# Two chained attentions and a mixture of four networks: PSUM in one pool of four double banks, sums of products made by a unit of their own, attention early in each pair, first loads reordered

## The chip, the cores and the metric

The kernel runs on one core of one Trainium2 chip. The time is device microseconds (us), the median of three runs. Beside it there is one profiled execution, from which all durations are read. A core has five engines with a queue each: TensorE (PE in the profile; its weight loads are PEld), VectorE (DVE), ScalarE (ACT), GpSimd (POOL) and SyncE (SP, which here only issues DMAs). Each engine works through its own queue in order.

## The reference

Eight batches of eight heads with 576 tokens of 64 values each. A packed attention of 32 queries `p` over `k` and `v` gives 32 packed rows per head; the tokens `q` then attend to these rows, which are keys and values at once. The result, as a matrix `x` of 4608 x 512, goes through four two-layer networks weighted per token:

```python
p_packed = sm_attn(p, k, v)
out = sm_attn(q, p_packed, p_packed)
...
p = domain_probs / (domain_probs.sum(-1, keepdims=True) + 1e-09)
for e in range(E):
    h = np.maximum(x @ w1[e], 0.0)
    out += p[:, e:e + 1] * (h @ w2[e])
```

Everything is float32. D is 512, the hidden width F is 1024, E is 4.

## The kernel before

**Units.** Batches go in four pairs (`sb`). The hidden widths of the four networks are cut into eight channels of 512 (`ch`). A unit is one channel of one batch, 64 in all, in the order pair, channel, even batch, odd batch. The loop at the end runs over them.

**A unit.** Its main work is seven products (`product`, `ORDER`): h @ w2 with hidden blocks and weights combined by Strassen-Winograd rules, so that seven products of blocks replace eight. A product is 12 matmuls of 288 columns into a double PSUM bank. Float32 precision comes from splitting each operand into a rounded part (hi, an ACT cast) and a rest (lo, a POOL subtraction), and three matmuls per block. Four groups of 12 matmuls (`mm1_group`) make the hidden blocks `ablk` of the next unit; DVE takes them out of PSUM with the relu and the token's weight (L299). `s_operand` makes the combined blocks `sblk` (DVE, L316) and the split operand `st`, two products ahead. Each product is taken out of PSUM by DVE and added to one of seven sums `acc` (L382), in channel 0 copied by ACT (L380).

**The end of a pair.** In the last channel `finish` (L391) also combines the seven sums to the four blocks of the output: seven additions of two sums each, all on DVE and right behind the product that they need, and four stores.

**Attention.** `pack_unit` (two pairs of heads of the packed attention; four packs per pair of batches) loads k and v, makes scores on PE (`kt,pbd`), the maximum on DVE (L158), the exponential on ACT (L162), transposes it on PE (L70), multiplies with v (`vt,at`), scales (L188), transposes (`ident,ppn`) and writes the packed rows `ppbd`. `tok_unit` (also four per pair) makes the tokens' scores (`kt,ppbd`), a softmax over 32 entries on DVE and ACT (L219 to L233), and the split result `xh`, `xl`. Attention of the next pair runs beside the units of this pair: packs in the even units of channels 1 to 4, tokens in the even units of channels 5 and 6 and in both units of channel 7. `g_form` multiplies w1 with the packed rows (`wraw,ppbd`), so that mm1 needs only the attention weights `xh`, `xl`.

**First pair.** `t_form` makes the combined and split blocks of w2 of the next channel in the odd units of the first pair, and `t_store` puts them into DRAM; later pairs load them back. Before the loop, attention of batches 0 and 1, the first w1 and w2 and the first mm1 run as a start-up.

**PSUM.** Eight banks: three double buffers `dbl` (mm1, products, scores) and two single buffers `aux` (transposes, products with v, g_form).

**Order.** The program is recorded in the order of the code; a scheduler with a simulated timeline then sets the order of each engine's queue. `together` forces the matmuls of one g_form behind all PE work recorded before it.

Of the kernel before, what the change touches and what calls it, by code (L numbers as in the profile page):

```python
# [16 lines left out]
P = 128  # L17
# [21 lines left out]
def attention_moe(ctx: ExitStack, tc: tile.TileContext, q, k, v, p, dp, w1, w2, out):  # L39
# [7 lines left out]
    xpool = pool("xpool", 3)  # L47
# [4 lines left out]
    ps_aux = pool("ps_aux", 2, space=PSUM)  # L52
    ps_dbl = pool("ps_dbl", 3, space=PSUM)
# [28 lines left out]

    def aux():
        return ps_aux.tile([P, 512], F32, name="aux")
# [32 lines left out]
    def norm_probs():  # L117
        pb = const.tile([P, E, TP], F32, name="pb")
        nc.sync.dma_start(out=pb, in_=dp)
# [7 lines left out]
        nc.sync.dma_start(out=pnd.rearrange("e (p t) -> p e t", p=P), in_=pb)  # L127

    def pack_unit(b, g, new):
        pd = pbd[b % 2]  # L130
        if g == 0:
            pt = small.tile([P, NPAIR, NPK], F32, name="pt", bufs=1)
            nc.sync.dma_start(out=pt, in_=p[b])
            for hh in range(2):
                nc.gpsimd.tensor_copy(
                    out=pd[hh * D:(hh + 1) * D, :, hh * NPK:(hh + 1) * NPK], in_=pt[hh * D:(hh + 1) * D]
                )
        kt = new([P, 2, S], "kt")
        nc.sync.dma_start(out=kt, in_=k[b][:, 2 * g:2 * g + 2, :])
        vt = new([P, len(SC), 4 * D], "vt")  # L140
# [30 lines left out]
        ps = aux()  # L171
        for c in range(nfull):
            tr(out=ps[:, c * P:(c + 1) * P], in_=a1[:, c * P:(c + 1) * P], identity=ident)
        nc.scalar.copy(out=at[:, 0:nfull, :], in_=ps.rearrange("p (c s) -> p c s", s=P))
        ps = aux()
        r = S - nfull * P
        tr(out=ps[0:r, 0:P], in_=a1[:, nfull * P:S], identity=ident)
        nc.scalar.copy(out=at[0:r, nfull, :], in_=ps[0:r, 0:P])
        yield
        ps = aux()  # L180
        for c, (_, n) in enumerate(SC):
            for h in range(4):
                mm(
                    out=ps[h * NPK:(h + 1) * NPK, 0:D], lhsT=at[0:n, c, h * NPK:(h + 1) * NPK],
# [3 lines left out]
        nc.vector.tensor_scalar_mul(ppn, ps[:, 0:D], rs)  # L188
        yield
        ps = aux()  # L190
        tr(out=ps[0:D, 0:P], in_=ppn, identity=ident)
        psv = ps[0:D, 0:P].rearrange("p (j h n) -> p j h n", j=2, h=2)
# [9 lines left out]
    def tok_unit(b, g, new):  # L202
# [20 lines left out]
        nc.vector.tensor_tensor(out=a2, in0=a2, in1=m2.broadcast_to([P, S // 32, NPK]), op=ALU.subtract)  # L223
# [6 lines left out]
        nc.vector.tensor_tensor(out=a2, in0=a2, in1=s2.broadcast_to([P, S // 32, NPK]), op=ALU.mult)  # L230
# [18 lines left out]
    def g_form(bs, ch, raws):  # L249

        for g in range(NG):
            pss = {b: aux() for b in bs}
# [11 lines left out]
            for b in bs:  # L264
                ghl = gpool.tile([P, 2, FC], F32R, name="ghl", bufs=6)
# [68 lines left out]
    def t_form(ch, new, eng):  # L334
# [15 lines left out]
        for i, name in enumerate(ORDER):  # L350
            n = of[name]
            if n in how:
                t = new([P, 2, DH], {"t1": "at", "t2": "a1", "t3": "a1", "t4": "at"}[n])
                eng.tensor_tensor(out=t, in0=blk[how[n][0]], in1=blk[how[n][1]], op=ALU.subtract)
# [9 lines left out]
    def product(u, i):  # L364
# [16 lines left out]
        elif ch < NCH - 1:  # L381
            nc.vector.tensor_tensor(out=accs[b, i], in0=psv, in1=accs[b, i], op=ALU.add)  # L382
        else:
            finish(b, ORDER[i], psv)

    def finish(b, name, psv):
# [6 lines left out]
        def store(t, r, n):  # L393
            nc.sync.dma_start(
                out=out[n * DH:(n + 1) * DH, b * S + r * HS:b * S + (r + 1) * HS].rearrange("(j p) t -> p j t", p=P),
                in_=t,
            )

        t = m[name]
        if name == "a22":  # L400
            add(t, m["s3"], t, ALU.subtract)
            add(t, t, psv, ALU.subtract)
            store(t, 1, 0)
# [5 lines left out]
        elif name == "s2":  # L409
# [4 lines left out]
            store(m["s1"], 1, 1)  # L414
        elif name == "s4":
            store(t, 0, 1)
        elif name == "a12":
            store(t, 0, 0)
# [26 lines left out]
    with ExitStack() as first:  # L445
# [10 lines left out]
        toks = [tok_unit(b, g, unit_tile(2 * b + g)) for b in range(2) for g in range(NG)]  # L456
        forms = t_form(0, form_tile, nc.gpsimd)
        for i in range(2):
            next(packs[i])
        raws = w1_load(0)  # L460
        for i in range(2):
            next(packs[i])
        for i in range(2):
            next(toks[i])
        for i in range(2, 4):
            next(packs[i])
        norm_probs()
        next(forms)
        drain(wavefront(packs[:2], 1))
        for b in range(2):  # L470
            load_probs(b, 0)
        drain(g_form([0], 0, raws))
        drain(wavefront(toks[:2], 1))
# [97 lines left out]
```

## Time and profile before

| | |
|---|---|
| median of 3 runs | 1380.16 us (1379.9 to 1381.48) |
| the profiled execution's own time | 1386.64 us |
| its span, first to last instruction | 1384.9 us |
| DVE, ACT, POOL busy | 71%, 34%, 58% of the span |
| DMA | 208.92 MB, 44.5% of 16 engines on the hardware queue |

All terms below are of the profiled execution, which took 6.5 us longer than the median of the other runs; its time lies 1.7 us above its span. A line of the profile names the source line (L67 is the helper that records every matmul), the engine, the operation, what it writes and reads, and how often. Names in brackets behind a row give the idle time before it and what ended it. L67, L70 and L75 are helpers, so that the tile names tell groups apart: `dbl<-st,tt` is a product, `dbl<-xl,ghl` and `dbl<-xh,ghl` are mm1, `aux<-wraw,ppbd` is g_form. PE is clocked down at times: PEclk is the share of full speed.

### The profile page before, as it was taken

To read this page: it belongs to the slowest core of one execution; us is meant where nothing else is said; L and a number is where in the kernel's file an instruction comes from. 1 tells how busy PE (TensorE), PEld (TensorE's weight loads), DVE (VectorE), ACT (ScalarE), POOL (GpSimd) and SP (SyncE) were. 2 spreads that over 40 slices of the span, in tenths; PEclk is the share of its full clock that TensorE was granted. 3 is DMA by queue.
4 is the path that set the end of the run, shared out by engine and by line. 5 is a ranking of instruction groups with operands and counts; after the bars stand their busy time and mean duration, and the time that the engine had idled before them with its cause. 6 is when DMAs were issued, how large, how long until landed. Compare 5 with 4: busy or idle time off the path is not lost.

```text
span 1384.9 us, 26088 instructions
## 1 busy us (share of the span) xinstructions
PE 1312.6 (95%) x10464; PEld 1192.3 (86%) x10464; DVE 984.0 (71%) x1380; ACT 475.0 (34%) x786; POOL 804.0 (58%) x548
## 2 busy tenths in 40 slices
PE   5699999999889999999998999999998899999997
PEld 2488898888888889899987998889997799999997
DVE  4757778788994666667798466666779656666668
ACT  2354343434325333233323433333332342332331
POOL 2656887777846445555645544455565455555555
PEclk9789999999999999999999999999999999999999
DMA  8525454444553444444445443445444344443421
GB/s 279 209 94 176 169 183 168 166 166 143 182 188 122 144 145 158 157 159 144 132 152 174 133 164 135 133 139 163 148 146 151 111 145 132 146 146 131 138 92 69
DMA packets 84630, 208.92 MB, mean 151 GB/s; under 512 B 8608, under 2 KB 27168, under 8 KB 84512
## 3 DMA queue, kind: packets, MB, share of 16 engines
q1 hardware_dynamic: 84512, 207.27, 44.5%
q8 instruction: 83, 1.36, 0.4%
q14 instruction: 35, 0.29, 0.1%
HBM read 168.37 MB, written 38.87 MB: 150 GB/s over the span
## 4 chain that ended last, share of the span: by engine, by line
PE 76%; DVE 16%; DMA 3%; issue 2%; POOL 1%; ACT 1%; DVEq 0%; SPq 0%; ACTq 0%
PE dbl L67 71%; DVE acc L391 5%; PE aux L75 4%; DVE sblk L316 4%; DVE ablk L299 2%; DMA kt<-in_w 1%; DVE ghl L115 1%; DVE acc L382 1%; DVE a L223 1%; DMA pb<-in_dp 1%; POOL xl L115 1%; PE aux L70 1%; DMA kt<-in_q 1%; DVE s L227 0%; DVE a L219 0%
## 5 line engine op out<-in xcount | busy, mean ns | idle before, releaser
L67 PEld LDWEIGHTS dbl<-st,tt 128*128 128x128 f32 x5376 | 736.1, 189 | 93.1 <-issue 61.4
L67 PE MATMUL dbl<-st,tt 128*128 128x288 f32 x5376 | 791.3, 299 | 23.2 <-DVE acc L391 6.6
L115 POOL TENSOR_TENSOR st<-sblk,st 128x576 fp32r<-128x576 f32 x256 | 397.7, 1559 | 292.3 <-ACT st L110 288.5
L67 PE MATMUL dbl<-xh,ghl 128*128 128x288 f32 x2048 | 419.8, 297 | 0.0
L115 POOL TENSOR_TENSOR st<-ablk,st 128x576 fp32r<-128x576 f32 x192 | 286.3, 1491 | 228.4 <-ACT st L110 193.1
L67 PEld LDWEIGHTS dbl<-xh,ghl 128*128 128x128 f32 x2048 | 333.4, 191 | 0.0
L299 DVE SCALAR_TENSOR_TENSOR ablk<-dbl,pbt 128x576 f32<-128x576 f32 x256 | 192.6, 752 | 188.8 <-PE dbl L67 188.7
L67 PE MATMUL dbl<-xl,ghl 128*128 128x288 f32 x1024 | 306.5, 299 | 17.3 <-POOL xl L115 15.5
L382 DVE TENSOR_TENSOR acc<-dbl,acc 128x576 f32<-128x576 f32 x336 | 253.2, 754 | 90.3 <-PE dbl L67 89.4
L110 ACT CAST st<-sblk 128x576 fp32r<-128x576 f32 x256 | 173.0, 676 | 356.3 <-DVE sblk L316 232.3
L110 ACT CAST st<-ablk 128x576 fp32r<-128x576 f32 x192 | 129.7, 675 | 261.6 <-PE dbl L67 241.2
L67 PEld LDWEIGHTS dbl<-xl,ghl 128*128 128x128 f32 x1024 | 195.2, 191 | 20.1 <-POOL xl L115 16.7
L316 DVE TENSOR_TENSOR sblk<-ablk 128x576 f32<-128x576 f32 x128 | 116.0, 906 | 10.7 <-POOL st L115 0.5
L115 DVE TENSOR_TENSOR ghl<-aux,ghl 128x512 fp32r<-128x512 f32 x128 | 83.3, 684 | 53.1 <-ACT ghl L110 53.1
L75 PE MATMUL aux<-wraw,ppbd 64*32 64x512 f32 x1024 | 85.9, 621 | 1.9 <-DVE ppbd L195 1.8
L110 ACT CAST ghl<-aux 128x512 fp32r<-128x512 f32 x128 | 69.0, 588 | 49.9 <-PE aux L75 49.9
L316 DVE TENSOR_TENSOR sblk<-ablk,sblk 128x576 f32<-128x576 f32 x64 | 65.4, 1022 | 6.5 <-POOL st L115 0.8
L391 DVE TENSOR_TENSOR acc<-acc,acc 128x576 f32<-128x576 f32 x56 | 58.1, 1069 | 0.2
L316 DVE TENSOR_TENSOR sblk<-sblk,ablk 128x576 f32<-128x576 f32 x64 | 55.7, 871 | 2.0
L380 ACT COPY acc<-dbl 128x576 f32<-128x576 f32 x56 | 35.7, 639 | 57.3 <-PE dbl L67 57.3
L391 DVE TENSOR_TENSOR acc<-dbl,acc 128x576 f32<-128x576 f32 x48 | 35.4, 742 | 1.7 <-PE dbl L67 1.7
L75 PEld LDWEIGHTS aux<-wraw,ppbd 64*32 64x32 f32 x1024 | 14.3, 106 | 23.4 <-issue 15.5
(66 smaller groups left out, 496.2 us busy)
## 6 DMA issues: line engine op xcount, KB each, us to landing
tt<-td SPq DMA_DIRECT2D x168, 512.0 KB, 3.8
wraw<-in_w SPq DMA_DIRECT2D x128, 256.0 KB, 3.0
td<-tt SPq DMA_DIRECT2D x56, 512.0 KB, 2.6
kt<-in_k SPq DMA_DIRECT2D x16, 576.0 KB, 3.8
kt<-in_q SPq DMA_DIRECT2D x16, 576.0 KB, 3.6
pbt<-pnd SPq DMA_DIRECT2D x32, 288.0 KB, 3.9
out<-acc SPq DMA_DIRECT2D x32, 288.0 KB, 2.6
vt<-in_v SPq DMA_DIRECT2D x16, 512.0 KB, 3.8
```

The source lines that it names most:

```text
L67: on_pe(nc.tensor.matmul(**kw))
L70: on_pe(nc.tensor.transpose(**kw))
L75: ins = nc.tensor.matmul(**kw).ins
L110: nc.scalar.copy(out=dst, in_=src)
L115: eng.tensor_tensor(out=dst, in0=src, in1=hi.bitcast(F32), op=ALU.subtract)
L223: nc.vector.tensor_tensor(out=a2, in0=a2, in1=m2.broadcast_to([P, S // 32, NPK]), op=ALU.subtract)
L299: nc.vector.scalar_tensor_tensor(out=a, in0=ps[:, :, 0:HS], scalar=0.0, in1=pbt[b][:, ts].rearrange("p (o t) -> p o t", o=1).broadcast_to( ...
L316: nc.vector.tensor_tensor(out=t, in0=blk(x), in1=blk(y), op=op)
L380: nc.scalar.copy(out=accs[b, i], in_=psv)
L382: nc.vector.tensor_tensor(out=accs[b, i], in0=psv, in1=accs[b, i], op=ALU.add)
L391: nc.vector.tensor_tensor(out=dst, in0=x, in1=y, op=op)
```

## The change

- PSUM: one pool of four double buffers for everything. The transposes of one pack go into one of them, and both batches of one g_form share one; the split results `ghl` have five buffers in place of six.
- `finish` stays for the last batch alone. All others only add their products, and `combine` makes the seven additions of two sums, three on DVE and four on POOL, one behind each product of the unit that follows in the code.
- Attention: in the first pair one pack or token unit in every even unit (packs in channels 0 to 3, tokens in channels 4 to 7); in the second and third pair one in every unit from the third to the tenth. `x` has four buffers in place of three.
- g_form runs one product later, behind the mm1 group of that product. Of the first unit, the mm1 groups for unit 1 come behind products 4 to 6.
- Start-up: the token weights are normed first, their DMAs on ACT's queue; k of both packs ahead of v, w2 ahead of w1; the copies into `pbd` on ACT in place of POOL; one token unit's subtraction and scaling on POOL.
- `t_form`: the first of four subtractions of a channel on POOL in place of DVE.

```diff
-    ps_aux = pool("ps_aux", 2, space=PSUM)
-    ps_dbl = pool("ps_dbl", 3, space=PSUM)
+    ps_dbl = pool("ps_dbl", 4, space=PSUM)
...
     def norm_probs():
-        nc.sync.dma_start(out=pb, in_=dp)
+        nc.scalar.dma_start(out=pb, in_=dp)
...
     def pack_unit(b, g, new):
-                nc.gpsimd.tensor_copy(
+                nc.scalar.copy(
...
         nc.sync.dma_start(out=kt, in_=k[b][:, 2 * g:2 * g + 2, :])
+        yield
...
     def g_form(bs, ch, raws):
-            pss = {b: aux() for b in bs}
+            ps = dbl()
+            pss = {b: ps[:, b % 2] for b in bs}
...
     def product(u, i):
-        elif ch < NCH - 1:
+        elif ch < NCH - 1 or b < B - 1:
             nc.vector.tensor_tensor(out=accs[b, i], in0=psv, in1=accs[b, i], op=ALU.add)
         else:
             finish(b, ORDER[i], psv)
...
+    def combine(b):
+        m = {n: accs[b, i] for i, n in enumerate(ORDER)}
+        for eng, dst, x, y, op, to in (
+            (nc.vector, "s2", "s2", "a11", ALU.add, None),
+            (nc.gpsimd, "a12", "a12", "a11", ALU.add, (0, 0)),
+            (nc.vector, "s3", "s3", "s2", ALU.add, None),
+            (nc.gpsimd, "s4", "s4", "s1", ALU.add, None),
+            (nc.gpsimd, "s4", "s4", "s2", ALU.add, (0, 1)),
+            (nc.vector, "s1", "s1", "s3", ALU.add, (1, 1)),
+            (nc.gpsimd, "a22", "s3", "a22", ALU.subtract, (1, 0)),
+        ):
+            eng.tensor_tensor(out=m[dst], in0=m[x], in1=m[y], op=op)
+            if to is not None:
+                store(b, m[dst], *to)
+            yield
...
+        norm_probs()
+        for i in (0, 1, 0, 1):
             next(packs[i])
+        next(forms)
         raws = w1_load(0)
...
+    GROUPS_FIRST = {4: ((0, 0), (0, 1)), 5: ((1, 1),), 6: ((1, 0),)}
+    sums = nothing
...
-            if not odd and 1 <= ch <= 4:
-                back = pack_unit(nb + (ch - 1) // NG, (ch - 1) % NG, att_tile)
-            elif not odd and 5 <= ch <= 6:
-                back = tok_unit(nb, ch - 5, att_tile)
-            elif ch == 7:
-                back = tok_unit(nb + 1, b % 2, att_tile)
+        step = 2 * ch + b % 2
+        if sb + 1 < SB and (sb == 0 and not odd or sb > 0 and 2 <= step < 10):
+            x = ch if sb == 0 else step - 2
+            make = pack_unit if x < 4 else tok_unit
+            back = make(2 * sb + 2 + x % 4 // NG, x % NG, att_tile)
...
-            if i in (2, 5):
-                next(gsteps, None)
-            if nxt and i in GROUPS:
-                mm1_group(u + 1, *GROUPS[i])
+            if nxt:
+                for grp in (GROUPS if u else GROUPS_FIRST).get(i, ()):
+                    mm1_group(u + 1, *grp)
+            if i in (3, 6):
+                next(gsteps, None)
...
             next(back, None)
+            if i == 0:
+                next(back, None)
+            next(sums, None)
...
+        if ch == NCH - 1 and b < B - 1:
+            sums = combine(b)
```

**A pack on PE.** The first place is PE's queue in channel 1 of the second pair, where one pack runs. Before, from the last mm1 matmuls ahead of the pack's transposes (`ident,a`) to the product behind them; between the pack's scores and these rows lie a product, a g_form, a product and an mm1 group:

```order
L67 MATMUL dbl<-xl,ghl 128x288
L67 MATMUL dbl<-xh,ghl 128x288 x2
L67 MATMUL dbl<-st,tt 128x288 x6
L70 MATMUL aux<-ident,a_5169 128x128 x4
L67 MATMUL dbl<-st,tt 128x288
L70 MATMUL aux<-ident,a_5169 64x128
L67 MATMUL dbl<-st,tt 128x288 x5
```

And now, from the same kind of place on, with the scores (`kt,pbd`) in it:

```order
L66 MATMUL dbl<-xl,ghl 128x288
L66 MATMUL dbl<-xh,ghl 128x288 x2
L66 MATMUL dbl<-kt,pbd_83 64x288 x4
L66 MATMUL dbl<-st,tt 128x288 x12
L69 MATMUL dbl<-ident,a_5140 128x128 x4
L69 MATMUL dbl<-ident,a_5140 64x128
L66 MATMUL dbl<-st,tt 128x288 x12
```

Between a pack's scores and its transposes there is now one product, where two products, a g_form, an mm1 group and half a product were. All packs of the loop stand like this.

**The end of a pair on DVE.** The second place is DVE's queue in the even unit of the last channel of the second pair. Before, from the product s2 on (`acc_4759` is s2's sum; `a_8018` is the token unit's softmax):

```order
L391 TENSOR_TENSOR acc_4759<-dbl,acc_4759 128x576
L229 RECIPROCAL s_8102<-s_8102 128x18
L299 SCALAR_TENSOR_TENSOR ablk<-dbl,pbt 128x576
L391 TENSOR_TENSOR acc_4690<-acc_4690,acc_4759 128x576
L391 TENSOR_TENSOR acc_4827<-acc_4827,acc_4759 128x576
L230 TENSOR_TENSOR a_8018<-a_8018,s_8102 128x576
L316 TENSOR_TENSOR sblk<-ablk 128x576
L391 TENSOR_TENSOR acc_4794<-acc_4690,acc_4794 128x576
L391 TENSOR_TENSOR acc_4827<-acc_4827,acc_4725 128x576
L299 SCALAR_TENSOR_TENSOR ablk<-dbl,pbt 128x576
L233 STREAM_TRANSPOSE at<-a_8018 128x576
L391 TENSOR_TENSOR acc_4794<-acc_4794,dbl 128x576
```

And now, from the same product on (`acc_4709` is s2's sum; L429 is `combine`):

```order
L379 TENSOR_TENSOR acc_4709<-dbl,acc_4709 128x576
L429 TENSOR_TENSOR acc_4709<-acc_4709,acc_4632 128x576
L296 SCALAR_TENSOR_TENSOR ablk<-dbl,pbt 128x576
L429 TENSOR_TENSOR acc_4653<-acc_4653,acc_4709 128x576
L313 TENSOR_TENSOR sblk<-ablk 128x576
L111 TENSOR_TENSOR ghl<-dbl,ghl 128x512
L379 TENSOR_TENSOR acc_4760<-dbl,acc_4760 128x576
```

The token unit's rows are gone from here, and of the sums three are left on DVE. Though the code makes the sums in the following unit, the scheduler puts these three between the products of the same unit.

**The first unit on PE.** The third place is PE's queue where the loop begins. Before, from the first g_form of batch 1 on; the tokens' scores of batch 1 are `kt,ppbd`, and the first `xl` behind them is that of batch 1:

```order
L75 MATMUL aux<-wraw,ppbd_89 32x512 x8
L67 MATMUL dbl<-kt,ppbd_89 64x288 x8
L67 MATMUL dbl<-st,tt 128x288 x24
L67 MATMUL dbl<-xl,ghl 128x288
L67 MATMUL dbl<-xh,ghl 128x288 x2
L67 MATMUL dbl<-st,tt 128x288 x12
```

And now:

```order
L74 MATMUL dbl<-wraw,ppbd_86 32x512 x8
L66 MATMUL dbl<-kt,ppbd_86 64x288 x8
L66 MATMUL dbl<-st,tt 128x288 x24
L66 MATMUL dbl<-kt,pbd_83 64x288 x4
L66 MATMUL dbl<-st,tt 128x288 x12
L69 MATMUL dbl<-ident,a_715 128x128 x4
L69 MATMUL dbl<-ident,a_715 64x128
L66 MATMUL dbl<-st,tt 128x288 x12
```

Behind the tokens' scores stand first three products and the scores of a pack of batch 2, then the pack's transposes and, further on, a g_form and two more products; only then does the first `xl` of batch 1 follow.

More of the change, by code (lines that the diff above doesn't have):

```diff
@@ L187, in pack_unit @@
         ppn = small.tile([P, D], F32, name="ppn")
-        nc.vector.tensor_scalar_mul(ppn, ps[:, 0:D], rs)
+        nc.vector.tensor_scalar_mul(ppn, ps[:, 0, 0:D], rs)
         yield
-        ps = aux()
-        tr(out=ps[0:D, 0:P], in_=ppn, identity=ident)
-        psv = ps[0:D, 0:P].rearrange("p (j h n) -> p j h n", j=2, h=2)
+        ps = dbl()
+        tr(out=ps[0:D, 0, 0:P], in_=ppn, identity=ident)
+        psv = ps[0:D, 0, 0:P].rearrange("p (j h n) -> p j h n", j=2, h=2)
         prs = slice(2 * g, 2 * g + 2)
@@ L200, in attention_moe, with tok_unit @@
     xs = {}
-    def tok_unit(b, g, new):
+    def tok_unit(b, g, new, eng=nc.vector):
         if g == 0:
@@ L251, in g_form @@
         for g in range(NG):
-            pss = {b: aux() for b in bs}
+            ps = dbl()
+            pss = {b: ps[:, b % 2] for b in bs}
             calls = []
@@ L384, in product, with store @@
             finish(b, ORDER[i], psv)
+    def store(b, t, r, n):
+        nc.sync.dma_start(
+            out=out[n * DH:(n + 1) * DH, b * S + r * HS:b * S + (r + 1) * HS].rearrange("(j p) t -> p j t", p=P),
+            in_=t,
+        )
     def finish(b, name, psv):
@@ L455, in attention_moe @@
         packs = [pack_unit(b, g, unit_tile(2 * b + g)) for b in range(2) for g in range(NG)]
-        toks = [tok_unit(b, g, unit_tile(2 * b + g)) for b in range(2) for g in range(NG)]
-        forms = t_form(0, form_tile, nc.gpsimd)
-        for i in range(2):
+        toks = [
+            tok_unit(b, g, unit_tile(2 * b + g), nc.gpsimd if (b, g) == (0, 1) else nc.vector)
+            for b in range(2) for g in range(NG)
+        ]
+        forms = t_form(0, form_tile, {n: nc.gpsimd for n in ("t1", "t2", "t3", "t4")})
+        norm_probs()
+        for i in (0, 1, 0, 1):
             next(packs[i])
+        next(forms)
         raws = w1_load(0)
-        for i in range(2):
-            next(packs[i])
+        drain(wavefront(packs[:2], 1))
         for i in range(2):
             next(toks[i])
+        for i in (2, 3, 2, 3):
+            next(packs[i])
         for i in range(2, 4):
[L466 to L469, printed above, removed]
+            next(toks[i])
         for b in range(2):
             load_probs(b, 0)
+        for _ in range(3):
+            next(forms)
         drain(g_form([0], 0, raws))
         drain(wavefront(toks[:2], 1))
+        drain(forms)
         drain(wavefront(packs[2:], 1))
@@ L476, in attention_moe @@
             mm1_group(0, kh, c)
-        for i in range(2, 4):
-            next(toks[i])
         drain(g_form([1], 0, raws))
         raws = w1_load(1)
-        drain(wavefront([forms] + toks[2:], 1))
+        drain(wavefront(toks[2:], 1))
     apool = ctx.enter_context(tc.tile_pool(name="apool", bufs=2, reuse_waits="tile"))
@@ L509, in attention_moe @@
         forming = odd and sb == 0 and ch + 1 < NCH
-        tsteps = t_form(ch + 1, att_tile, nc.vector) if forming else nothing
+        tsteps = nothing
+        if forming:
+            tsteps = t_form(ch + 1, att_tile, {"t1": nc.gpsimd, "t2": nc.vector, "t3": nc.vector, "t4": nc.vector})
         next(tsteps, None)
@@ L532, in attention_moe @@
         drain(gsteps)
+        drain(sums)
+        if ch == NCH - 1 and b < B - 1:
+            sums = combine(b)
         if not odd:
```

45 lines of the change are left out of this document (17 added, 28 removed).

## The prediction

> **What bounds the kernel now.** First the page, for the busy shares:
>
> ```profile
> span 1384.9 us, 26088 instructions
> PE 1312.6 (95%) x10464; PEld 1192.3 (86%) x10464; DVE 984.0 (71%) x1380; ACT 475.0 (34%) x786; POOL 804.0 (58%) x548
> ```
>
> PE is busy 95%, so at most 72 us can come from filling its idle time, and something more where idle time brought a slower clock. Next the busy time by stage; a channel runs from one g_form to the same one of the next channel:
>
> ```profile
> core 0: us, PE busy (x) PEld busy (x) DVE busy (x) ACT busy (x) POOL busy (x), PEclk, DMA share, GB/s
> 0.00:87.20 87.20, 56.80 (x469) 40.21 (x469) 50.20 (x94) 29.83 (x56) 40.48 (x41) 0.84 0.60 207
> 86.20:433.01 346.81, 329.65 (x2624) 299.11 (x2631) 282.73 (x363) 136.38 (x230) 255.25 (x168) 0.99 0.47 164
> 629.74:668.59 38.85, 38.85 (x313) 36.05 (x319) 29.32 (x43) 12.65 (x20) 23.29 (x15) 1.00 0.46 147
> 668.59:756.72 88.13, 80.03 (x616) 72.49 (x623) 76.89 (x103) 28.73 (x46) 51.13 (x32) 1.00 0.48 160
> 796.76:838.53 41.77, 41.61 (x359) 37.54 (x364) 26.56 (x41) 13.14 (x24) 20.41 (x14) 1.00 0.45 150
> 1129.57:1167.10 37.53, 37.53 (x304) 35.52 (x311) 24.82 (x34) 11.61 (x18) 20.86 (x14) 1.00 0.42 135
> 1363.00:1385.00 22.00, 14.84 (x108) 14.42 (x108) 17.81 (x23) 3.70 (x6) 10.62 (x6) 0.90 0.31 107
> ```
>
> The row at 1129.57 is a plain channel: 37.53 us, PE without a gap. One with a token unit takes 38.85 (the row at 629.74), so that unit costs PE 1.32 and DVE 4.5 us. One with a pack takes 41.77 (796.76), so a pack costs PE 4.24. In these channels PE is the bound. The row at 668.59 holds the two channels that close the second pair: 88.13 us, where two plain ones and two token units would take 75.06 + 2.64 = 77.70. The excess is 10.4 us, and DVE is busy 76.89 of the 88.13. The first pair (86.20 to 433.01) takes 346.81 where eight channels, four packs and four token units make 300.24 + 16.96 + 5.28 = 322.5, an excess of 24.3. The stretch to 87.20 has 30 us of idle PE and a clock of 0.84.
>
> Then, who is waited for; these are the longest waits of PE:
>
> ```profile
> PE dbl L67 <- POOL xl L115: 15.5, 5, 7.6
> PE dbl L67 <- DVE acc L391: 7.3, 10, 1.6
> PE dbl L67 <- DVE ablk L299: 7.3, 7, 2.0
> PE dbl L67 <- DVE acc L382: 5.1, 2, 2.5
> ```
>
> The first is the start-up and the pairs' ends (token results late), the next two the ends of pairs (a PSUM buffer that DVE has not emptied), the last two stalls in the first pair.
>
> **The ends of pairs.** The additions and the emptying of PSUM on DVE, and the rests on POOL:
>
> ```profile
> L382 DVE TENSOR_TENSOR acc<-dbl,acc 128x576 f32<-128x576 f32 x336 | 253.2, 754 | 90.3 <-PE dbl L67 89.4
> L391 DVE TENSOR_TENSOR acc<-acc,acc 128x576 f32<-128x576 f32 x56 | 58.1, 1069 | 0.2
> L115 POOL TENSOR_TENSOR st<-sblk,st 128x576 fp32r<-128x576 f32 x256 | 397.7, 1559 | 292.3 <-ACT st L110 288.5
> ```
>
> Two channels at the end of a pair hold 2 x 24.82 us of plain DVE work, three token units of 4.5 (one is just begun at 668.59) and 14 additions of 1.07: 78 us, what DVE was busy. PE needs 77.70, and the work comes in bursts, so DVE sets the pace. Changed, the second and third pair have there 2 x 24.82 + 6 x 1.07 = 56 us of DVE work beside 75 us of PE. The excess of 10.4 should go but for about 1.4: **-9 us each, -18 for both**. Lower bound of the gain 5 (half stays as bursts), upper 10.4. What goes to POOL, 8 additions per pair at about 1.56, adds 12.5 us to two units in which POOL was busy 20.86 of 37.53: it fits, and the lateness of a rest that queues behind one addition (1.6) is covered by the two products that an operand is made ahead. What is late next is DVE's third addition, which waits for POOL's, with the next product's emptying behind it on DVE; four PSUM buffers cover about two products of it, over 3 us.
>
> In the first pair a token unit stays in the last channel's even unit and three follow channels in which w2 is formed. Its excess of 24.3 has a pair's end (about 11), the two stalls for `acc L382` and smaller waits. A stall costs more than its length:
>
> ```profile
> 300.69 1.76 PE L67 MATMUL dbl<-st,tt 128*128 128x288 f32 x12
> 305.00 2.96 PE L67 MATMUL dbl<-st,tt 128*128 128x288 f32 x12 [2.55 <-DVE acc L382]
> ```
>
> After 2.55 us of waiting, 12 matmuls take 2.96 us where 1.76 is usual, so a stall is worth about 4. The Trainium skill (TensorE: Matmul & The Clock Gate, "What's actually happening") has the clock fall only after an idle window of about 3.4 us, freely running; the trace has it fall after less, and by the page's number alone these two stalls would be worth 2.4 us less in this term. With one subtraction of w2 on POOL, a fourth PSUM buffer and the end relieved I take an excess of 14 left: **-10 us** (bounds -3 and -18: only a third of the end goes, or all but 6).
>
> **The start-up.** Before, in time order:
>
> ```profile
> 25.51 0.40 DVE L121 TENSOR_REDUCE psum_e<-pb 128x36 f32<-128x144 f32 x1 [1.64 <-DMA pb<-in_dp]
> 27.54 1.28 DVE L124 TENSOR_TENSOR pb<-pb,psum_e 128x144 f32<-128x144 f32 x1
> 9.01 2.19 PE L67 MATMUL dbl<-kt,pbd 128*64 128x288 f32 x8 [1.69 <-DMA kt<-in_k]
> 48.27 0.40 PE L67 MATMUL dbl<-xl,ghl 128*128 128x288 f32 x1 [1.96 <-POOL xl L115]
> 70.98 0.61 PE L67 MATMUL dbl<-xl,ghl 128*128 128x288 f32 x1 [7.55 <-POOL xl L115]
> ```
>
> The norming of the weights holds DVE from the wait at 23.87 to 28.82, while the token softmax of batch 0 stands behind it; put first, it runs while DVE waits for the first scores. That frees some 3.5 of the 5 us (the rest ran beside other waits). The second pack waits 1.69 for k behind v; now k comes first. Two of a token unit's additions with broadcast go from DVE to POOL, which finishes the forming of w2 first: 2 us off DVE, part of it lost to POOL's queue. Together the first mm1 comes about 6 us earlier and the wait of 1.96 goes. The wait of 7.55 gets three more products (1.6 each) and a pack (4.2) as cover, but a new one comes: the pack's transposes wait for an exponential that stands on ACT behind the casts of `xh`, hence behind DVE's whole token softmax. I count 3 of the 7.55 as gained. **-11 us**, bounds -4 (only norming and k) and -15 (all three waits).
>
> SP's queue loses two DMAs to ACT's at the front, where ACT has nothing to do. The copies into `pbd` on ACT cost two short ones per batch on an engine that is 34% busy. The k of the loop's first pack now queues on SP behind w1's four loads, which wait for the last g_form of the start-up; it lands near the second product, and the price is within the bounds above.
>
> **The packs' new wait.** One pack before, in the second pair:
>
> ```profile
> 459.67 1.19 PE L67 MATMUL dbl<-kt,pbd 128*64 128x288 f32 x8
> 460.79 1.86 PE L67 MATMUL dbl<-st,tt 128*128 128x288 f32 x12
> 460.90 0.76 DVE L158 TENSOR_REDUCE nb<-dbl 128x1 f32<-128x576 f32 x1 [0.37 <-PE dbl L67]
> 461.94 0.74 ACT L162 ACTIVATE a<-dbl,nb 128x576 f32<-128x576 f32 x1 [3.08 <-DVE nb L159]
> 462.58 0.19 ACT L162 ACTIVATION_READ_ACCUMULATOR a<-dbl,nb 128x1 f32 x1
> 462.58 1.09 PE L75 MATMUL aux<-wraw,ppbd 64*32 64x512 f32 x16
> ```
>
> The product behind the scores is done by 462.58 at the latest; the exponential ends at 462.77. Before, the transposes came some 5 us later and never waited in the loop. Now they stand right behind that product, so PE waits 0.25 to 0.4 us with DVE free as here. 12 packs at 0.4: **+5 us**. Upper bound: one emptying and one `sblk` (together 1.7) ahead of the maximum on DVE, 12 x 2 = +24; lower +1. Behind the waiting transposes on PE stand a product and mm1; nobody else waits.
>
> **Token units in a row.** In the second and third pair four units in a row have a token unit, and DVE then has 12.41 + 4.5 = 16.9 of 18.77 + 1.32 = 20.1 us, 84%. Before, alternate units had 75% without a wait. I take 0.4 each for eight: **+3 us**, bounds 0 and +12 (1.5 each, as the waits for `acc L391`).
>
> At nothing: the later g_form (its `ghl` is needed two products, 3.3 us, later, and ACT's cast and DVE's rest take about 2), the fifth `ghl` buffer, `x`'s fourth, the loads (DMA 42 to 48% busy), the tail (still `finish`, DVE 17.81 of 22.00 us; the bound is 1.5 either way). If g_form's cover were gone, each of 31 odd units would show a wait of up to 1 us.
>
> **Sum:** -18 - 10 - 11 + 5 + 3 = -31 us on the profiled execution's 1386.64; put on the median of 1380.16, 1349.
>
> **The rivals.**
> - *The locked additions.* POOL's additions and DVE's contend: two SBUF inputs on DVE take 1069 ns, one from PSUM 754. POOL's 28 additions add to that, and DVE's third waits for POOL's. If every POOL addition held a DVE operation for its own 1.56, 12.5 us per pair's end would come on top of DVE's 56, of which 19 us of slack take the larger part when spread, and little when in bursts. With half of the end's excess left in all pairs: +14, 1363. The Trainium skill (SBUF — State Buffer, "Who interferes with whom") says that a Vector instruction with two SBUF inputs and a GpSimd one that reads SBUF lock each other out for a whole instruction; the two means agree that there is contention, and this rule speaks against moving additions to POOL. Chance 0.17.
> - *Start-up only shifts its waits* from `xl` to the pack's exponential: -3 in place of -11, 1357. Chance 0.12.
> - *The packs' wait turns long* (the other side: slower). Should `sblk` and an emptying always stand ahead of the maximum and contend with POOL, the transposes come 2.5 us late, which drops the clock as at 305.00: some 4.5 us for each of 12 packs, +54 in place of +5, 1398. It decides from 3 us per pack, where 36 us undo the rest. Against it: in DVE's queue only the emptying of mm1 stands just ahead of the maximum. Chance 0.07.
> - *The change doesn't do what it says*: the order shows the sums in the same unit as their products, so DVE's third addition may stop a full DVE at the end of the first pair, where a token unit remains: +4, 1353. Chance 0.05.
> - *All idle time goes*: ends at nothing, the transposes' wait at 0.1: 1335. Chance 0.05.
>
> **How the numbers follow.** My forecast has 0.54, 1349, by itself 1338 to 1360. The range for 8 in 10 takes the best and worst bounds half together, 1332 to 1374. A measurement of this kernel tells 0.2% (2.8 us) from no change. Faster by more: all but the long wait of the packs and the worst of the locked additions, 0.89; within it 0.04; slower 0.07.
>
> **What would show it.** Right: no excess in the two channels that close the second and third pair (about 75 us, DVE under 65), no PE wait for `xl` behind the start-up, 12 short waits of the transposes for ACT `a`, the first mm1 near 38 us. Wrong: PE waiting for DVE in the token units or for POOL `st` at a pair's end, transposes that wait over 1 us, or a long wait for the pack's exponential in the first unit that gives the start-up back.

## The result and the profile after

| | before | changed |
|---|---|---|
| median of 4 runs | 1380.18 us (1379.9 to 1381.48) | 1338.69 us (1338.04 to 1342.07) |
| ratio, 95% interval | | 0.9703 (0.9685 to 0.972) |
| span of the profiled execution | 1384.9 us | 1337.2 us |

The forecast was 1349, its own range 1338 to 1360, so the time lies just inside its lower end. The first rows of the page:

```profile
span 1337.2 us, 26182 instructions
PE 1284.7 (96%) x10464; PEld 1181.2 (88%) x10464; DVE 993.8 (74%) x1343; ACT 480.0 (36%) x802; POOL 861.0 (64%) x569
...
PEclk8899999999999999999999999999999999999999
```

PE's busy time fell by 28 us and its idle time by 20. Where, the busy time by stretch tells. All stretches below end with the last product of a channel's odd unit, so that the same work lies between them in both kernels. First before, in this order: the first pair behind its first channel; the channel behind it; the two channels around the end of the second pair; the last channel with the tail:

```profile
106.56:412.74 306.18, 291.63 (x2323) 263.53 (x2322) 255.19 (x334) 113.86 (x192) 226.65 (x150) 0.98 0.49 170
412.74:453.38 40.64, 38.03 (x298) 35.59 (x298) 22.05 (x28) 19.64 (x33) 22.92 (x16) 1.00 0.42 136
698.16:787.49 89.33, 81.23 (x611) 72.86 (x610) 67.32 (x87) 32.30 (x53) 47.34 (x31) 0.98 0.46 153
1346.81:1384.80 37.99, 30.79 (x228) 30.14 (x227) 32.12 (x39) 7.43 (x11) 20.61 (x12) 0.94 0.21 73
```

Then the changed kernel, with the start-up and first channel as its first row and a channel with two packs as its fourth:

```profile
0.00:97.24 97.24, 72.83 (x668) 57.67 (x669) 61.60 (x110) 46.80 (x90) 55.63 (x46) 0.89 0.61 219
97.24:396.15 298.91, 281.01 (x2268) 256.43 (x2268) 265.27 (x317) 111.22 (x194) 245.08 (x159) 1.00 0.49 170
396.15:433.68 37.53, 37.53 (x298) 35.53 (x298) 20.33 (x24) 19.31 (x32) 27.34 (x19) 1.00 0.49 163
433.68:477.66 43.98, 43.68 (x406) 39.06 (x406) 27.58 (x47) 15.93 (x29) 20.53 (x15) 1.00 0.56 176
677.00:752.61 75.61, 75.32 (x595) 71.09 (x594) 52.02 (x61) 30.28 (x49) 55.87 (x37) 1.00 0.49 165
1296.85:1337.10 40.25, 32.11 (x229) 31.63 (x227) 31.23 (x35) 7.33 (x11) 26.39 (x16) 0.95 0.20 69
```

Read against each other:

| stretch | before | changed | difference |
|---|---|---|---|
| start-up and first channel (now with a pack) | 106.56 | 97.24 | -9.3 |
| rest of the first pair (now with a pack less) | 306.18 | 298.91 | -7.3 |
| the channel behind it | 40.64 | 37.53 | -3.1 |
| end of the second pair, two channels; the third the same | 89.33 | 75.61 | -13.7 each; -2.6 of that two token units moved away |
| a pack in the second and third pair | 4.24 | (43.98 - 37.53) / 2 = 3.23 | -1.0, eight times |
| last channel and tail | 37.99 | 40.25 | +2.3 |

With the moved token units put back into the ends (11.1 each) this makes -9.3 - 7.3 - 3.1 - 22.2 - 8.1 + 2.3 = -47.7, the difference of the spans. The medians differ by 41.5 only: the profiled execution of before was 6.5 us longer than its median. In which stretch these 6 us lie isn't known, so some of the differences are too large by as much in all. Last, who is waited for by PE:

```profile
PE dbl L69 <- ACT a L159: 17.2, 11, 8.6
PE dbl L66 <- DVE acc L379: 10.0, 7, 1.8
PE dbl L66 <- DMA kt<-in_k: 6.4, 2, 5.6
PE dbl L66 <- POOL st L111: 6.3, 4, 3.2
```

The waits for `xl` are gone from the top; the first row is the transposes' new wait, 8.6 us of it in the first unit and 5.3 in the start-up. The second row is new: PE waiting for DVE's emptying, all seven times in token units of the first pair. The longest of the last row stands in the last channel.

### The profile page after: what moved, and what is told of

Read it like the earlier page. It is cut to its first block, busy times and chain, and to the rows that moved or that the text cites. A ratio compares the mean times of both kernels' runs of the same rounds, so it can differ in the third digit from the quotient of the medians.

```text
span 1337.2 us, 26182 instructions
## 1 busy us (share of the span) xinstructions
PE 1284.7 (96%) x10464; PEld 1181.2 (88%) x10464; DVE 993.8 (74%) x1343; ACT 480.0 (36%) x802; POOL 861.0 (64%) x569
## 4 chain that ended last, share of the span: by engine, by line
PE 66%; DVE 6%; issue 1%; POOL 1%; ACT 1%; DVEq 0%; ACTq 0%
PE dbl L66 62%; PE dbl L74 3%; DVE sblk L313 1%; DVE acc L394 1%; DVE ablk L296 1%; DVE acc L379 1%; DVE acc L429 1%; POOL acc L429 1%; PE dbl L69 1%; ACT a L159 1%; DVE nb L155 0%; DVE ghl L111 0%; POOL st L111 0%; DVE a L351 0%; DVE a L219 0%
## 5 line engine op out<-in xcount | busy, mean ns | idle before, releaser
L66 PE MATMUL dbl<-st,tt 128*128 128x288 f32 x5376 | 777.2, 298 | 14.1 <-DVE acc L379 6.9
L379 DVE TENSOR_TENSOR acc<-dbl,acc 128x576 f32<-128x576 f32 x385 | 289.4, 752 | 103.0 <-PE dbl L66 101.1
L313 DVE TENSOR_TENSOR sblk<-ablk 128x576 f32<-128x576 f32 x128 | 133.3, 1042 | 10.3
L106 ACT CAST ghl<-dbl 128x512 fp32r<-128x512 f32 x128 | 75.0, 586 | 156.3 <-PE dbl L74 79.5
L111 DVE TENSOR_TENSOR ghl<-dbl,ghl 128x512 fp32r<-128x512 f32 x128 | 87.8, 686 | 21.1 <-ACT ghl L106 18.0
L313 DVE TENSOR_TENSOR sblk<-ablk,sblk 128x576 f32<-128x576 f32 x64 | 71.0, 1110 | 8.5 <-POOL st L111 2.2
L74 PE MATMUL dbl<-wraw,ppbd 64*32 64x512 f32 x1024 | 71.9, 605 | 0.0
L429 POOL TENSOR_TENSOR acc<-acc,acc 128x576 f32<-128x576 f32 x28 | 47.4, 1701 | 17.5 <-DVE acc L379 17.5
L111 POOL TENSOR_TENSOR xl<-at,xh 128x576 fp32r<-128x576 f32 x16 | 28.0, 1754 | 15.7 <-ACT xh L106 15.7
L429 DVE TENSOR_TENSOR acc<-acc,acc 128x576 f32<-128x576 f32 x21 | 30.6, 1459 | 4.8 <-POOL acc L429 4.6
```

The costliest lines, as they stand in the source:

```text
L66: on_pe(nc.tensor.matmul(**kw))
L74: ins = nc.tensor.matmul(**kw).ins
L106: nc.scalar.copy(out=dst, in_=src)
L111: eng.tensor_tensor(out=dst, in0=src, in1=hi.bitcast(F32), op=ALU.subtract)
L313: nc.vector.tensor_tensor(out=t, in0=blk(x), in1=blk(y), op=op)
L429: eng.tensor_tensor(out=m[dst], in0=m[x], in1=m[y], op=op)
```

## The experiments

Each kernel was timed beside the kernel before on the same chip. The median of before lay between 1381.2 and 1384.6 us there, so medians are compared as ratios to it. Stretches are compared by their spans in the one profiled execution; what a span gains on the 1384.9 of before is too large by the 6 us named above.

### What freed the ends of pairs

Three parts could have: the moved token units, the sums, the fourth double buffer. **The sums undone:**

```diff
-        elif ch < NCH - 1 or b < B - 1:
+        elif ch < NCH - 1:
...
-        if ch == NCH - 1 and b < B - 1:
+        if False:
             sums = combine(b)
```

> The changed kernel with the sums made as before, in the last channel by DVE, for all batches; nothing else is undone. If the prediction's account holds (token units and additions together fill DVE at the ends of pairs), DVE now has 2 x 24.82 + 14 x 1.07 = 65 us there beside 75 us of PE, in bursts: some 2 to 5 us of waits come back at each of the four ends, 1346 to 1358. If moving the token units alone empties DVE enough, the ends stay without waits and the last pair is free of the two POOL additions that stood ahead of an operand's rest at 1319.84 (PE waited 3.20): 1335 to 1338. If POOL's additions slow DVE at every end (locked), it is faster by more, below 1334.

Ratio 0.9685 (0.9671 to 0.97), span 1338.8, where the changed kernel has 0.9703 and 1337.2: the intervals overlap, so this is the second case, and neither a gain nor a loss is shown. **Only the sums**, in the kernel before:

```diff
-        elif ch < NCH - 1:
+        elif ch < NCH - 1 or b < B - 1:
...
+            next(sums, None)
...
+        if ch == NCH - 1 and b < B - 1:
+            sums = combine(b)
```

> The kernel before with only the sums changed (three additions on DVE, four on POOL). If the additions filled DVE at the ends, 4 of 7 per batch gone take most of three excesses: -15 to -27, 1353 to 1365. If the token units decide, each end gives 2 to 3 us and the last pair loses 2: -4 to -7, 1373 to 1376. The sum made without interaction: what this run and the one with only the attention moved gain adds up to the ends' gain of the change, 33 us with the first pair.

0.9908 (0.9893 to 0.9923), span 1369.9, 15 us less; by the medians it is 12.9 less, which lies between the two cases. **Attention at its old places**, all else changed:

```diff
-            x = ch if sb == 0 else step - 2
-            make = pack_unit if x < 4 else tok_unit
-            back = make(2 * sb + 2 + x % 4 // NG, x % NG, att_tile)
+            if not odd and 1 <= ch <= 4:
+                back = pack_unit(nb + (ch - 1) // NG, (ch - 1) % NG, att_tile)
+            elif not odd and 5 <= ch <= 6:
+                back = tok_unit(nb, ch - 5, att_tile)
+            elif ch == 7:
+                back = tok_unit(nb + 1, b % 2, att_tile)
```

> The changed kernel with packs and token units at their old places in the pairs; sums, PSUM, start-up and g_form as changed. At an end of a pair DVE then has 2 x 24.82 of plain work, 3 token units of 4.5 and three additions of 1.46 per batch, about 72 us, beside 77.7 us of PE. If the token units are what filled DVE, about half of the excess of 10.4 to 11.6 us comes back at each of three ends, 1354 to 1370. If the additions were, the ends stay nearly free of waits: 1338 to 1344.

0.9812 (0.9797 to 0.9827), span 1356.0: the first case. **Only attention moved**, in the kernel before:

```diff
-    xpool = pool("xpool", 3)
+    xpool = pool("xpool", 4)
...
-                ghl = gpool.tile([P, 2, FC], F32R, name="ghl", bufs=6)
+                ghl = gpool.tile([P, 2, FC], F32R, name="ghl", bufs=5)
...
+        if sb + 1 < SB and (sb == 0 and not odd or sb > 0 and 2 <= step < 10):
+            x = ch if sb == 0 else step - 2
+            make = pack_unit if x < 4 else tok_unit
```

> The kernel before with only packs and token units moved (and the buffers of x and ghl that this needs); PSUM, sums and start-up as before. If the token units decide: the ends of the second and third pair lose 9 to 11 us each, the first pair's end 3 to 5, while the pack in the first unit gives 0 to +5: 1353 to 1363. If the additions decide, -5 to -10: 1370 to 1375. If the two single PSUM buffers matter for packs in neighbouring units, the g_form behind each pack's transposes waits as before (0.9 us each).

0.9812 (0.9792 to 0.9832), span 1356.0: the first case too. The two channels around the second pair's end, of these four in this order:

```profile
680.17:756.04 75.87, 75.29 (x594) 71.08 (x594) 54.67 (x69) 30.06 (x49) 45.26 (x29) 1.00 0.51 165
```
```profile
692.90:776.28 83.38, 79.03 (x610) 72.25 (x610) 59.27 (x79) 32.24 (x53) 60.42 (x39) 1.00 0.49 164
```
```profile
677.06:762.82 85.76, 79.45 (x610) 72.25 (x610) 65.41 (x79) 32.12 (x53) 57.98 (x39) 1.00 0.47 159
```
```profile
689.30:769.26 79.96, 77.35 (x594) 72.64 (x594) 55.67 (x69) 29.98 (x49) 44.12 (x29) 0.98 0.49 156
```

Plain work there is 75.06 us, with two token units (second and third row) 75.06 + 2.64 = 77.7. So the excess, 11.6 before and 0.55 in the changed kernel, is 0.8 without the sums, 5.7 with the sums alone, 8.1 with the tokens left where they were, 4.9 with the tokens alone moved. For the fourth buffer the two runs on PSUM below have the same stretch: 76.54 us with the old PSUM and all else changed, an excess of 1.5, and 91.54 with the pooled PSUM alone, an excess of 13.8. So the tokens must go, and one of the other two with them; the sums alone take half; and with the tokens gone and PSUM pooled the sums take 0.3 us. Across the whole kernel they pay at the first pair's end alone (its last channel 47.83 without them, 44.08 with them) and cost in the last:

### The last channel

**The old form of the end for both batches of the last pair**, sums elsewhere:

```diff
-        elif ch < NCH - 1 or b < B - 1:
+        elif ch < NCH - 1 or b < B - 2:
...
-        if ch == NCH - 1 and b < B - 1:
+        if ch == NCH - 1 and b < B - 2:
```

> The changed kernel, but both batches of the last pair use the old form of the end (all seven additions on DVE); the three earlier pairs keep theirs. In the last channel PE waited 3.20 us for an operand's rest on POOL, behind two additions of 1.9 each. Theory: these two are the cause, so the last channel takes 31.7 in place of 35.3, of which the tail gives 1.5 back: -2, 1335 to 1336. Rival: DVE is then late instead (14 additions of 1.07 beside 24.8 of plain work in 32 us): 0 to +2.

Ratio 0.9675 (0.9648 to 0.9701), which overlaps with the changed kernel's; the span is 1334.7, and the last channel with the tail is back to 38.12 us:

```profile
1296.48:1334.60 38.12, 30.60 (x229) 30.13 (x227) 30.63 (x39) 7.33 (x11) 21.01 (x12) 0.98 0.21 74
```

In the changed kernel the timeline shows the two additions on POOL, then the rest, then PE's product:

```profile
1319.84 3.83 POOL L429 TENSOR_TENSOR acc<-acc,acc 128x576 f32<-128x576 f32 x2
...
1323.63 1.91 POOL L111 TENSOR_TENSOR st<-ablk,st 128x576 fp32r<-128x576 f32 x1
...
1325.59 4.58 PE L66 MATMUL dbl<-st,tt 128*128 128x288 f32 x21 [3.20 <-POOL st L111]
```

The last unit has no mm1 beside its products, so PE needs its operands faster than elsewhere, and 3.83 us ahead of a rest were more than the two products' lead covers.

### What made a pack cheaper

**PSUM as before** (three double buffers, two single ones for transposes, products with v and g_form), all else changed:

```diff
-    ps_dbl = pool("ps_dbl", 4, space=PSUM)
+    ps_aux = pool("ps_aux", 2, space=PSUM)
+    ps_dbl = pool("ps_dbl", 3, space=PSUM)
...
-            ps = dbl()
-            pss = {b: ps[:, b % 2] for b in bs}
+            pss = {b: aux() for b in bs}
```

> The changed kernel with three double buffers and two single ones again, the single ones for transposes, products with v and g_form as before. All else as changed. Theory: the pooled PSUM makes a pack cheaper, because g_form behind a pack's last transposes had to wait inside itself for its second single buffer (two of its weight loads in the trace of before start 0.75 us late), and it makes the ends of pairs free, because PE runs a buffer further ahead of DVE: 12 packs x 1 us and two to four ends of 2 to 4 us, +16 to +26, 1353 to 1363. Rival: the packs are cheaper because their transposes now stand in one run and no product is split around them: then +0 to +6, 1337 to 1343, and a pack still costs 3.2 us.

Ratio 0.9704 (0.9679 to 0.973), span 1341.1. **Only PSUM changed**, the same lines the other way round in the kernel before:

> The kernel before with only PSUM changed: four double buffers for everything. Theory as for the run that undoes it: packs cost 3.2 in place of 4.24 us (-12 for twelve) and each end loses 2 to 4 us: -16 to -26 on the span of 1384.9, 1359 to 1369. Rival (order, not PSUM): -0 to -6 with packs at 4.2.

0.9912 (0.9885 to 0.9939), span 1366.2. The channel with two packs and the end of the second pair, of the first; then start-up and first channel, a channel with one pack and the end of the second pair, of the second:

```profile
432.71:476.50 43.79, 43.79 (x406) 39.33 (x406) 27.57 (x47) 15.63 (x29) 20.47 (x15) 1.00 0.56 177
677.62:754.16 76.54, 75.79 (x594) 71.12 (x594) 50.84 (x61) 30.31 (x49) 55.73 (x37) 1.00 0.50 163
```
```profile
0.00:100.25 100.25, 71.94 (x614) 57.09 (x615) 63.59 (x106) 42.75 (x78) 55.96 (x52) 0.88 0.60 206
440.79:481.23 40.44, 40.44 (x353) 37.28 (x352) 25.92 (x40) 13.77 (x23) 20.80 (x15) 1.00 0.52 162
680.25:771.79 91.54, 81.63 (x610) 73.33 (x610) 64.99 (x87) 32.35 (x53) 46.60 (x31) 0.96 0.47 150
```

A pack costs 3.13 us with the old PSUM in the new order, 2.91 with the pooled PSUM in the old order, 4.24 with both old. For the packs either is enough. Undoing PSUM costs 3.9 us of the span and nothing by the ratios (0.9704 against 0.9703), as the theory of the order had it. PSUM alone gains 18.7 by the spans, but 12.4 by the medians, which lies between the two forecasts; it gains by packs and start-up and not by the ends. The place of the attention isn't all that the order does: in the kernel with only attention moved, the channel with two packs takes

```profile
444.09:489.17 45.08, 44.55 (x407) 39.35 (x406) 27.36 (x47) 15.20 (x27) 21.05 (x17) 1.00 0.56 172
```

which is 3.8 us a pack. What was dear shows in the timeline of before, in the pack that the prediction read, some 10 us further on:

```profile
473.57 0.30 PE L70 MATMUL aux<-ident,ppn 128*64 128x128 f32 x1 [0.15 <-DVE ppn L188]
473.80 2.00 PE L75 MATMUL aux<-wraw,ppbd 64*32 64x512 f32 x16
```

The g_form behind the pack's last transposes takes 2.00 us where the one at 462.58 takes 1.09. PE's weight loads waited inside it, by the view of waits for the transposes (L70), whose single buffer it takes next. The timeline of all engines shows that DVE's copies out of that buffer end at 474.57, and the loads go on at 474.68:

```profile
474.13 0.44 DVE L195 COPY ppbd<-aux 64x64 f32<-64x64 f32 x2
...
474.68 0.21 PEld L75 LDWEIGHTS aux<-wraw,ppbd 64*32 64x32 f32 x14 [0.75 <-PE aux L70]
```

In the whole kernel before, the view of waits counts nine of these:

```profile
PEld aux L75 <- PE aux L70: 6.3, 9, 0.8
```

In the changed kernel the g_form of the same pack takes 1.09, and the transposes wait 0.18:

```profile
443.13 0.76 PE L69 MATMUL dbl<-ident,a 128*128 128x128 f32 x5 [0.18 <-ACT a L159]
...
447.01 1.09 PE L74 MATMUL dbl<-wraw,ppbd 64*32 64x512 f32 x16
```

With only attention moved, the g_form right behind the first pack's transposes still takes 1.96 us (at 464.89), and the second pack, in the odd unit, has none behind it. With the old PSUM and all else changed, three mm1 matmuls stand between the transposes at 455.38 and the g_form at 455.98, which takes 1.39. So of the new order it is the later g_form that spares the stall.

The pooled PSUM alone gained little at the ends because another wait took the place of the old ones. PE got through its products sooner and then waited for the tokens, as long as the token units stayed in the last channel:

```profile
407.94 0.61 PE L66 MATMUL dbl<-xl,ghl 128*128 128x288 f32 x1 [6.79 <-POOL xl L114]
```

Such a wait was 1.99 us before; at the second pair's end the two channels took 91.54 us, more than the 89.33 of before.

### The start-up and the token units' step

**The start-up of before**, with all that came with it: the loads, the norming, the copies on POOL, and one step of attention behind the first product in place of two:

```diff
             next(back, None)
-            if i == 0:
-                next(back, None)
```

> The changed kernel with the start-up of before: token weights normed later and on SP's queue, the old order of the loads, copies into pbd on POOL, no second step of attention behind the first product, mm1 of the first unit at its old places. The first channel took 106.56 us before and 97.24 after, though it now holds a pack of about 3.2. Prediction's size: +11, 1350. If the start-up only shifts its waits: +3, 1342. By the channel's times, like for like: +12.5, 1351.

Ratio 0.9685 (0.9658 to 0.9712), span 1333.9: no slower than the changed kernel. None of the three sizes held, for two effects cancel:

```profile
0.00:102.36 102.36, 75.71 (x668) 59.25 (x669) 60.76 (x112) 44.49 (x82) 57.44 (x53) 0.90 0.62 208
102.36:392.55 290.19, 280.21 (x2268) 256.39 (x2268) 252.33 (x317) 110.98 (x190) 244.48 (x162) 1.00 0.51 175
```

The start-up is 5.1 us longer, the rest of the first pair 8.7 shorter. So **only the second step taken from the token units**, which puts all their work one product later:

```diff
-            if i == 0:
+            if i == 0 and make is pack_unit:
                 next(back, None)
```

> The changed kernel, but token units make one step behind the first product in place of two, so that all their work comes one product later; packs still make two. The run with the old start-up did this too, and its first pair took 290.2 us behind the first channel, against 298.9. Theory: it is this step that cost the first pair, because a token unit's scores and its work on DVE then lie beside the even unit's fullest stretch on DVE (PE waited 1 to 1.8 us for DVE's emptying in each of channels 4 to 7): the first pair behind its first channel takes 290 to 293, -6 to -9 on the changed kernel, 1329 to 1333. Rival: the old start-up's copies into pbd on POOL, or the order in which the first units leave it, made that difference: 297 to 299, no change.

Ratio 0.9644 (0.9625 to 0.9663), clear of the changed kernel's interval, and the first pair behind its first channel takes 290.85:

```profile
98.10:388.95 290.85, 280.22 (x2268) 256.38 (x2268) 251.46 (x317) 112.68 (x194) 244.07 (x159) 1.00 0.51 175
```

DVE runs the same 317 instructions in 251.46 us instead of 265.27, and PE's waits for `acc L379` fall from 10.0 us to 0.9. The groups of DVE in channels 4 to 7 of the first pair show half of that growth, 7 us, in the softmax's subtraction and scaling, first in the changed kernel, then a product later:

```profile
L219 DVE TENSOR_TENSOR a<-a,m 128x576 f32<-128x576 f32 x4 | 7.6, 1904 | 0.0
L226 DVE TENSOR_TENSOR a<-a,s 128x576 f32<-128x576 f32 x4 | 5.6, 1411 | 0.1
```
```profile
L219 DVE TENSOR_TENSOR a<-a,m 128x576 f32<-128x576 f32 x4 | 3.2, 804 | 0.0
L226 DVE TENSOR_TENSOR a<-a,s 128x576 f32<-128x576 f32 x4 | 3.0, 754 | 0.1
```

And the timeline of channel 5 in the changed kernel, DVE and POOL, shows why:

```profile
277.84 1.90 DVE L219 TENSOR_TENSOR a<-a,m 128x576 f32<-128x576 f32 x1
```
```profile
277.69 1.43 POOL L111 TENSOR_TENSOR st<-ablk,st 128x576 fp32r<-128x576 f32 x1
279.07 1.96 POOL L111 TENSOR_TENSOR st<-sblk,st 128x576 fp32r<-128x576 f32 x1
```

A product later, in the same channel:

```profile
277.47 0.81 DVE L219 TENSOR_TENSOR a<-a,m 128x576 f32<-128x576 f32 x1
```
```profile
277.62 1.96 POOL L111 TENSOR_TENSOR st<-ablk,st 128x576 fp32r<-128x576 f32 x1
```

Whichever starts first runs at its own length; the other ends 0.6 (DVE) or 1.3 us (POOL) after the first has ended, nearly its own length. DVE began 0.15 us behind POOL, and its 0.8 became 1.90: POOL's rest ended at 279.12, DVE at 279.74. In the kernel with the later step DVE began first, and POOL's 1.43 became 1.96. So it goes in all four token units: DVE's subtraction takes 1.89 to 1.92 us where it starts 0.13 to 0.15 behind POOL, and 0.80 to 0.81 where it starts as much ahead. That is a lock for whole instructions, and the Trainium skill (SBUF — State Buffer, "Who interferes with whom") says just this of a Vector instruction with two SBUF inputs beside a GpSimd one that reads SBUF; the trace agrees. The prediction weighed that rule for the additions at the ends, and it hit the token units of the first pair, where DVE is busy 265.27 of 298.91 us. How much of the gain is the lock, and how much the new order on DVE, isn't separated.

### The pack of the first unit

PE stood 8.63 us before the transposes of this pack. **The pack begun four products later:**

```diff
+            if u == 0:
+                back = chain(iter([None] * 4), back)
```

> The changed kernel with the pack of the first unit begun four products later. In the changed kernel PE stood 8.63 us before this pack's transposes while five products of the unit had their place around them. Theory: the exponential is late because it stands behind the whole token softmax, and two products and a g_form that now stand behind the transposes can run in that time; the wait moves to the tokens' xl at about 62.4 and shrinks to some 5 to 6 us: -3 to -6, 1333 to 1336. Rival: xl is late by as much, so that the wait is only renamed: 0 to -1.

Ratio 0.9687 (0.9665 to 0.9708), span 1335.9; the start-up and first channel took 96.69 us, half a microsecond less. The expected gain didn't come. Five products and a g_form stood ahead of the tokens' `xl` now, but PE stopped behind four products, at the g_form:

```profile
58.76 1.33 ACT L106 CAST xh<-at 128x576 fp32r<-128x576 f32 x2 [3.99 <-DVE at L229]
...
60.00 2.25 ACT L377 COPY acc<-dbl 128x576 f32<-128x576 f32 x4
...
60.68 1.96 PE L74 MATMUL dbl<-wraw,ppbd 64*32 64x512 f32 x16 [7.36 <-ACT acc L377]
```

In channel 0 ACT empties PSUM, and its copies stood in its queue behind the tokens' casts, which wait for DVE's softmax. Four buffers filled, and PE waited nearly as long as before.

### Together

**Later token units and the old end for the last pair**, both edits as above:

> The changed kernel with token units one step later and the old form of the end for the last pair; the first unit's pack stays where the change put it. Theory: the two add up (7.2 of the span for the token units, 2.1 to 2.5 for the last pair): span 1327 to 1328, some 0.7% below the changed kernel, 1329 to 1331. If the pack of the first unit were worth moving, this stands 1 us or more above the run with all three edits (1330.9); if that edit only renames a wait, the two are level.

1331.88 us, ratio 0.964 (0.9613 to 0.9666), span 1327.9. The span is what the two edits should give together, but this profiled execution was the shortest of five, and the median lies above the 1329 to 1331 expected: that they add up isn't shown. **With the first unit's pack moved as well**, the three edits above:

> The two edits above and the old form of the end for both batches of the last pair, together. Theory: the three touch different stretches (first unit, token units of the first pair, last channel) and add up: 1337.2 - 6 to 9 - 3 to 6 - 2.5 = 1320 to 1326. Rival: what the first unit gains is given back in the first pair, 1327 to 1331.

1330.9 us, ratio 0.9635 (0.9612 to 0.9659), short of the 1320 to 1326 expected. The medians of this one, of the one above and of the later token units alone (1332.58) can't be told apart; that moving the pack gains anything isn't shown. Later token units are the one single edit that is clearly faster than the changed kernel.

## Why the prediction came out as it did

The direction was right, and the time lies in the range by 0.7 us. The sum of -31 was too small: the medians differ by 41.5, and by the spans, on which its terms were read, by 47.7. That the time still lies in the range is in part luck: the terms were read from an execution 6.5 us longer than the median and then put on the median; the -47.7 put there would give 1332.5, outside. Of the rivals, *All idle time goes* (1335, chance 0.05) came nearer than the forecast: the ends' excess is 0.55, and behind the first unit no pack waits more than 0.2 us, close to what it had.

- **Ends of pairs, -18:** measured -22.2 (11.1 each). The place and the engine were right: DVE is busy 52.02 of 75.61 us, and the excess is gone. The share of the sums was not: the prediction took token units and sums as one term, and with the tokens moved and PSUM pooled the runs give the sums about 0.3 us of each of these two ends, though 5.9 alone in the kernel before. The working's 56 us of DVE were those of the last two channels; the 52.02 are of the last and the one behind it, where ACT copies the products. Without the sums it is 54.67, and with a fourth buffer PE hardly notices (an excess of 0.8).
- **Start-up -11 and first pair -10:** measured together -19.7 with the channel behind. Like for like, with the pack of 3.2 that the first channel now holds, the start-up gained 12.5 and the rest 7.2, so the sizes are near, but the cause was half missed. All edits of the start-up together are worth 5.1, and the pooled PSUM 6.3 (106.56 to 100.25 in the run with PSUM alone), which this term had at nothing. The wait for the pack's exponential came as said, 8.63 where `xl` had been waited for 7.55: the rival "start-up only shifts its waits" is right for this wait.
- **Packs' wait, +5:** the step that failed. The wait is there as worked out, but near its lower bound: behind the first unit, 0.18 us in seven packs and nothing in four. The rows read for it (a product done by 462.58, an exponential by 462.77) give that 0.19; 0.4 was taken. What the term left out is that a pack of before held a stall: 4.24 us was taken as PE's cost because PE's idle time showed nothing, while 0.9 us stood inside the g_form at 473.80, counted as busy. The eight packs of the second and third pair gave 8 us where +3 was in the sum.
- **Token units in a row, +3:** nothing. PE has no wait in any token unit of the second and third pair.
- **Tail, at nothing:** +2.3, for POOL's two additions ahead of the rest. The wait "behind one addition" was named and taken as covered by two products of lead; two additions stood there.
- **The locked additions, a rival at 0.17:** the lock is real. DVE's three additions take 1459 ns where the seven took 1069, POOL's 1701. At the ends it cost nothing visible; in the first pair's token units it is part of the 7.2 us by which the span with later token units is shorter (the two groups above hold 7 us of DVE's time), a place where no term had looked, since a step of the attention was read as order, not as what would meet on two engines.

## What to carry to other kernels

A group's duration can hold a stall that no idle time shows: compare the same group at two places before its time is taken as a cost. Where several edits free one bottleneck, undo each by itself; here the moved token units with either of the other two did for two ends, and the sums paid at one place and cost at another. When work moves by one step, look at what the other engine has under way at that moment, for two engines that lock each other out can lose more than the step gains.

## What was not expected of the hardware

A wait of 2 us halves PE's clock or leaves it, for the same wait at the same place. In the kernel with only attention moved, the product behind the second and behind the third pair's wait:

```profile
719.71 3.22 PE L67 MATMUL dbl<-st,tt 128*128 128x288 f32 x12 [1.99 <-DVE acc L391]
...
1044.55 1.83 PE L67 MATMUL dbl<-st,tt 128*128 128x288 f32 x12 [1.98 <-DVE acc L391]
```

The granted clock is 0.50 in the first 1.7 us of the first row's product (719.70 to 721.41), and over 13 us that begin before each wait's end it is 0.87 and 1.00:

```profile
717.00:730.00 13.00, 10.54 (x67) 10.13 (x66) 10.89 (x13) 2.02 (x3) 4.97 (x4) 0.87 0.52 195
1041.80:1054.80 13.00, 10.44 (x77) 10.02 (x76) 12.28 (x16) 2.02 (x3) 6.35 (x4) 1.00 0.60 224
```

The Trainium skill (TensorE: Matmul & The Clock Gate, "What's actually happening") has the gate watch windows of 3413 ns that run freely. That the two rows differ fits windows that do not start with the wait; that a wait of 1.99 us is enough does not fit a window idle throughout, and there the measurement decides. In the changed kernel no wait between the first unit and the last channel reached 2 us (the longest is 1.82), and the clock over that stretch (97.24 to 1296.85) was 1.00, which is part of what the first pair gained: the row at 106.56 has 0.98, that at 97.24 has 1.00.
